# A recurrent scan feeding two layers of experts: units one iteration earlier, their lists counted at step 1 and made in fewer steps

## The chip, the cores and the metric

One core of one Trainium2 chip runs the whole program. The metric is the device time of one execution in microseconds (us): the median of several executions. The core's engines are TensorE (PE in the rows; PEld is its weight loading), VectorE (DVE), ScalarE (ACT), GpSimd (POOL) and SyncE (SP, which here issues DMA transfers). Each works through its own queue in order and waits on the others by semaphores.

## What is computed

A gated recurrence over four sequences of 5056 tokens with 256 channels, then two layers of experts. In the first layer only tokens with a positive score are sent to an expert, in the second all are.

```python
# scan
f = lower_bound + (1 - lower_bound) * sigmoid(f_logit)
for t in range(S):                       # S = 5056, B = 4, D = 256
    h = f[:, t] * h + (1 - f[:, t]) * x[:, t];  y[:, t] = h
# layer 1, N = B*S = 20224 tokens, 8 experts, F = 1024
go = x @ w_skip > 0
e  = argmax(x[go] @ w_gate);  g = softmax(x[go] @ w_gate)[e]
out[go] = x[go] + g * (relu(x[go] @ w1[e]) @ w2[e]);  out[~go] = x[~go]
# layer 2, all tokens
e  = argmax(x @ w_gate2);  g = softmax(x @ w_gate2)[e]
out = g * (relu(x @ w1b[e]) @ w2b[e])
```

## The kernel before

**Chunks and iterations.** The scan runs over 40 chunks of 512 tokens, in a software pipeline of iterations `i` of four steps `s` = 0 to 3 (`side` and `work`). In an iteration VectorE scans a chunk (`scan2`, line 856), TensorE turns one to token rows (`turn`, line 880) and multiplies one by the gates' weights (`logits`, line 908; 923 and 926 from chunk 20 on), and every second iteration a group of eight tiles of 128 tokens is routed (`route`, odd iterations) and placed (`place`, even iterations): TensorE ranks the group's tokens within their experts (`ps_rank`), VectorE adds the group to the running count of tokens per expert (line 985), and GpSimd scatters the rows to a region per expert in memory (line 274), two tiles a step.

**Units.** A unit is 256 tokens of one expert (128 for the last, small ones). `Moe.step(k)` is a quarter of a unit: four steps make one, `k = 4u + f`. In step f TensorE does 12 products of the first matrix (`mm1`, line 609: hidden block f, in three half-precision parts) and, for the hidden block of two steps before, 12 of the second (`mm2`, lines 637 to 639). ScalarE and VectorE split each hidden block in two halves (`hh` line 620, `hl` line 621). At f = 2 the next unit's rows are transposed (`xpose`: `ps_x` line 596, then `xh` line 597 on ScalarE and `xl` line 598 on VectorE); at f = 3 the rows of the unit after that are loaded by SyncE (`load`, line 564). A unit's last `mm2` is done at f = 1 of the next, and VectorE then adds it to the rows (`finish1`, line 645). The step ends with `side(k)`, a quarter of an iteration of the scan, at s = f. Before unit 0 the scan runs alone for `I0` iterations; after the scan the units run alone. There are 126 units in all.

**Lists.** Which rows a unit takes is computed on the chip. At iteration 12, 16, 20, ... 40 `lists_of_scan(e)` starts list e with four units each. `count` multiplies the running count by ones (line 326, `ps_c`), so that every partition has the sum, and VectorE takes it over (line 329). Lists 0 and 1 then need two instructions (lines 535, 536); lists 2 to 7 some 20 small ones on tiles of 8 numbers (lines 407 to 493), a product with ones (`ps_b`, line 499) and two copies (501, 507). These steps are slipped in between the scan's instructions: `tick` after a step of a generator of `work`, the rest at a step's end by `listing`, up to `LS[s]` of them in step s; products only in steps named in `PS`. `state.cnt` in `count` is whatever count line 985 made last.

**Queues and buffers.** All orders are the order in which the program is written. `ps_x`, `ps_t`, `ps_l`, `ps_c` and `ps_b` share one pool of two PSUM buffers (`pt`), and `ps_o` of `mm2` a pool of three. Experts' weights are loaded and split meanwhile by `weights`, on the two schedules `WI`/`WS` before unit 0 and two a iteration after; the last eight quarters (from number 24 on) go over GpSimd (line 191).

**After the scan** (iteration 42, step 3) the small lists of layer 1 are made, rows of finished units are sorted into the regions of layer 2 and scattered by GpSimd (`sort_some`), and units run on.

Of the kernel before, what the change touches and what calls it, by code (L numbers as in the profile page):

```python
# [31 lines left out]
NU = (NT + E * (UT - 1)) // UT  # L32


I0, LN, NEARLY, K1A, K1B = 16, 4, 8, 6, 4
K2E, K2A, K2B = 8, 70, 6
NFIX = E // LN
NSCAN = LN * NEARLY * UJ
# [5 lines left out]
DL, DB, UF, KL = 2, 3, 5, 11  # L44

WQ = [(e, k) for e in range(E) for k in (2, 3)] + [(e, k) for e in range(E) for k in (0, 1)]
WI, WS, WD = [1, 2, 1] * 5 + [1], [1, 3], 0
WL = 17
WT = 24
LG, LB, LA1 = 4, 3, 1  # L50
CK, CS = 4, 3
KS, KX = 7, 3
CF = 20
LA, LF = 2, 3
LS = (8, 8, 10, 10)
PS = (3, 0, 1)

WB, LT, LT2, UW = 2, 6, 5, 4
# [36 lines left out]
def moe_chain(ctx: ExitStack, tc: tile.TileContext, xT, fT, lb, wg, w1a, w2a, w1b, w2b, out):  # L95
# [646 lines left out]
    with ExitStack() as ph:  # L742
# [677 lines left out]
        def side(k):  # L1420

            i, s = divmod(k + 4 * I0, 4)
            if k == -KS:
                moe.begin(units, n)
                moe.start()
            GL.n = LS[s]
            if i < nchunk + 3:
# [93 lines left out]
```

## Time and profile before

| | us |
|---|---|
| median of three executions (1580.51 to 1587.67) | 1583.88 |
| the profiled execution, its own time | 1587.33 |
| its span, first to last instruction | 1585.6 |
| TensorE busy in the span | 1498.6 |
| VectorE busy | 925.5 |
| ScalarE busy | 725.0 |
| GpSimd busy | 507.9 |

The span falls into three parts. Up to 140 us the scan runs alone, 140 to about 510 us scan and units run together, and from there on only units and sorting. TensorE is the engine with the most work. A gap in its row is time lost only where no other part of the program makes up for it, so its gaps are looked up one by one with what ended them. A row of the timeline gives the start in us from the span's begin, the duration, the engine, the line and the operation, and in brackets how long the engine stood idle before and what released it; rows of equal instructions that follow each other are merged (x2).

### The profile page before, as it was taken

The numbers are of one execution on the slowest core, as the hardware profiler recorded it, in microseconds if no ns is written. First come the engines' busy times: TensorE is split into PE (matmuls) and PEld (weight loads), VectorE is DVE, ScalarE is ACT, GpSimd is POOL, SyncE is SP. The second block draws the span as 40 slices with busy tenths as digits, with TensorE's granted clock in tenths as the row PEclk, the third lists the DMA queues.
The fourth block names the chain that finished last, engine by engine and source line by source line (L and its number), as shares of the span: only waits on it lengthen the run. The fifth ranks groups of instructions, "written<-read, shape, count | busy, mean of one in ns | idle before, by whom it ended". The sixth has DMA issues, their size and how long they took to land. (4 is left out here: it accounts for less than half of the span.)

```text
span 1585.6 us, 41240 instructions
## 1 busy us (share of the span) xinstructions
PE 1498.6 (95%) x13900; PEld 1346.4 (85%) x13901; DVE 925.5 (58%) x1947; ACT 725.0 (46%) x1419; POOL 507.9 (32%) x511
## 2 busy tenths in 40 slices
PE   5878989999999998999999999999999999999996
PEld 5877868888988887887888998998989989989985
DVE  5877677888885865546755555544444444444442
ACT  6777567776763232333344443433333333333332
POOL 1663455646453177016111111111111111111121
PEclk9988989999999999999999999999999999999998
DMA  8876655777774377327333323111111111111110
GB/s 289 274 266 212 212 178 201 260 243 252 242 253 153 103 232 244 121 71 243 110 100 103 97 98 106 50 49 56 49 50 57 47 51 50 49 54 49 49 48 22
DMA packets 127221, 213.73 MB, mean 135 GB/s; under 512 B 14459, under 2 KB 87807, under 8 KB 124464
## 3 DMA queue, kind: packets, MB, share of 16 engines
q1 hardware_dynamic: 107824, 157.51, 31.5%
q0 software_dynamic: 19200, 53.53, 9.2%
q8 instruction: 132, 2.16, 0.6%
q14 instruction: 65, 0.53, 0.1%
HBM read 120.10 MB, written 70.80 MB: 120 GB/s over the span
## 5 line engine op out<-in xcount | busy, mean ns | idle before, releaser
L621 DVE SCALAR_TENSOR_TENSOR hl<-ps_m,hh 128x512 f16<-128x512 f32 (+1 forms) x504 | 336.9, 668 | 554.6 <-ACT hh L620 553.1
L620 ACT ACTIVATE hh<-ps_m 128x512 f16<-128x512 f32 (+1 forms) x504 | 292.2, 580 | 634.8 <-PE ps_m L609 527.3
L637 PE MATMUL ps_o<-wt,hh 128*128 (+2 forms) x1936 | 531.7, 275 | 8.4 <-DVE rows L645 8.4
L638 PE MATMUL ps_o<-wt,hh 128*128 (+2 forms) x1936 | 531.8, 275 | 0.0
L639 PE MATMUL ps_o<-wt,hl 128*128 (+2 forms) x1936 | 531.7, 275 | 0.0
L609 PE MATMUL ps_m<-xh,w1s 128*128 128x256 f16 (+1 forms) x2880 | 505.9, 267 | 0.0
L609 PEld LDWEIGHTS <-w1s 128*128 128x128 f16 x4320 | 406.7, 98 | 45.5 <-issue 0.4
L274 POOL DMA_INDIRECT out_dram<-rows,dest x162 | 157.6, 973 | 750.1 <-ACT rows L681 636.8
L609 PE MATMUL ps_m<-xl,w1s 128*128 128x256 f16 (+1 forms) x1440 | 378.6, 267 | 0.0
L638 PEld LDWEIGHTS <-hh 128*128 128x128 f16 x1936 | 190.0, 98 | 33.5 <-issue 9.3
L609 PE MATMUL ps_m<-xh,wt 128*128 128x256 f16 x1152 | 215.9, 276 | 2.4 <-DVE hl L621 2.4
L639 PEld LDWEIGHTS <-hl 128*128 128x128 f16 x1936 | 190.1, 98 | 25.0
L637 PEld LDWEIGHTS <-hh 128*128 128x128 f16 x1936 | 190.0, 98 | 22.6
L274 POOL DMA_INDIRECT regions<-rw,dest x158 | 175.9, 1113 | 91.9 <-issue 42.5
L609 PEld LDWEIGHTS <-wt 128*128 128x128 f16 x1728 | 168.8, 99 | 23.8 <-issue 3.1
L609 PE MATMUL ps_m<-xl,wt 128*128 128x256 f16 x576 | 158.7, 276 | 0.0
L583 DVE COPY w1s<-wt 128x4096 f16 x90 | 110.8, 1231 | 11.6 <-issue 4.8
L274 POOL DMA_INDIRECT regions<-wt,b_dest x80 | 84.7, 1059 | 42.2 <-issue 17.9
L856 DVE TENSOR_TENSOR_SCAN xt<-ft,end,xt 128x512 f32<-128x512 f32 (+4 forms) x78 | 94.9, 1246 | 0.4
L598 DVE SCALAR_TENSOR_TENSOR xl<-ps_x,xh 128x512 f16<-128x512 f32 (+1 forms) x126 | 83.1, 660 | 16.7 <-ACT xh L597 16.6
L596 PE MATMUL ps_x<-ident,rows 128*128 128x128 f32 x484 | 75.0, 276 | 18.2 <-DMA rows<-regions 18.2
L681 ACT ACTIVATE rows<-ps_o,rows 128x256 f32<-128x256 f32 x162 | 68.3, 471 | 33.2 <-PE ps_o L639 33.2
(241 smaller groups left out, 1317.1 us busy)
## 6 DMA issues: line engine op xcount, KB each, us to landing
rows<-regions SPq DMA_DIRECT2D x116, 272.0 KB, 2.8
wt<-wt SPq DMA_DIRECT2D x20, 1024.0 KB, 6.0
ft<-in_fT_dram SPq DMA_DIRECT2D x39, 512.0 KB, 4.0
xt<-in_xT_dram SPq DMA_DIRECT2D x39, 512.0 KB, 4.9
wt<-mid SPq DMA_DIRECT2D x40, 272.0 KB, 4.5
mid<-rows SPq DMA_DIRECT2D x38, 272.0 KB, 3.6
wt<-in_w2a_dram SPq DMA_DIRECT2D x16, 512.0 KB, 4.7
wt<-in_w1a_dram SPq DMA_DIRECT2D x16, 512.0 KB, 3.9
```

Of the source, the lines that this page charges most:

```text
L274: r = nc.gpsimd.indirect_dma_start(out=dst, out_offset=bass.IndirectOffsetOnAxis(ap=idx_ap, axis=0), in_=rows_ap, in_offset=None, bounds_c ...
L583: nc.vector.tensor_copy(t.w1, wt[:, bass.ds(o, W2O)])
L596: nc.tensor.transpose(ps[:, d, j * P : (j + 1) * P], t.rows[:, j, d * P : (d + 1) * P], ident)
L598: nc.vector.scalar_tensor_tensor(out=t.xl, in0=ps, scalar=SX, in1=t.xh, op0=ALU.mult, op1=ALU.subtract)
L609: nc.tensor.matmul(ps[:, f, :], lhsT=t.w1[:, wo : wo + P], rhs=x[:, d, :], start=f == 0 and k == 0, stop=f == 1 and k == 5, skip_group_che ...
L620: nc.scalar.activation(hh, ps, AF.Relu)
L621: nc.vector.scalar_tensor_tensor(out=hl, in0=ps, scalar=0.0, in1=hh, op0=ALU.max, op1=ALU.subtract)
L637: nc.tensor.matmul(ps, lhsT=hh[:, f, js], rhs=hi, start=first, stop=False)
L638: nc.tensor.matmul(ps, lhsT=hh[:, f, js], rhs=lo, start=False, stop=False)
L639: nc.tensor.matmul(ps, lhsT=hl[:, f, js], rhs=hi, start=False, stop=last)
L681: nc.scalar.activation(y, t.ps[j][:, :D], AF.Copy, scale=t.rows[:, j, CGATE : CGATE + 1])
L856: nc.vector.tensor_tensor_scan(x[:, d, s0:s1], f[:, d, s0:s1], x[:, d, s0:s1], init, ALU.mult, ALU.subtract)
```

## The change

Four constants are changed, and the shape of one.

```diff
-I0, LN, NEARLY, K1A, K1B = 16, 4, 8, 6, 4
+I0, LN, NEARLY, K1A, K1B = 15, 4, 8, 6, 4
...
-WI, WS, WD = [1, 2, 1] * 5 + [1], [1, 3], 0
+WI, WS, WD = [1, 2, 1] * 5, [1, 3], 0
...
-CK, CS = 4, 3
+CK, CS = 3, 1
...
-LS = (8, 8, 10, 10)
+LS = (12, 12, 12, 12)
```

`I0`: unit u runs in iteration 15 + u instead of 16 + u; all that hangs on a unit (its load, its transposition, the lists after the scan, the sorting) keeps its place relative to the unit or to the iteration as the code has it. `WI` loses the entry of iteration 15, which now follows the schedule of iterations with units: two quarters of weights are handled in it instead of one, and all later ones one call earlier. `CK`, `CS`: list e is begun in the same iteration, 12 + 4e, but at step 1 instead of step 3; its first unit is in iteration 15 + 4e instead of 16 + 4e. At step 1 of these iterations line 985 has just been issued, so the same groups are counted as before. `LS`: up to 12 instead of 8 or 10 list steps in a step.

The first units on TensorE. Before, the count's transposed unit rows (`ps_x`) and the first `mm1` of unit 0 (`ps_m`) stand behind the gates' product `ps_l` of chunk 13:

```order
L233 MATMUL ps_rank<-oh,ones 128x128
L1037 MATMUL ps_v<-wgt,wt 128x48 x8
L880 MATMUL ps_t<-ident,xt 128x128 x8
L908 MATMUL ps_l<-wgt,xt 128x102 x8
L596 MATMUL ps_x<-ident,rows 128x128 x4
L880 MATMUL ps_t<-ident,xt 128x128 x8
L609 LDWEIGHTS wt
L609 MATMUL ps_m<-xh,wt 128x256
```

with the change:

```order
L233 MATMUL ps_rank<-oh,ones 128x128
L1037 MATMUL ps_v<-wgt,wt 128x48 x8
L596 MATMUL ps_x<-ident,rows 128x128 x4
L880 MATMUL ps_t<-ident,xt 128x128 x8
L609 LDWEIGHTS wt
L609 MATMUL ps_m<-xh,wt 128x256
```

The product `ps_l` of that chunk now stands behind the first step of unit 0, and one iteration of the scan that had no unit beside it has one.

The count on TensorE in iteration 24, the fourth of eight (`ps_c` is the count, the rows with `waits` name the semaphore that is waited for). Before, it stands at the end of step 3, behind the gates' product:

```order
L926 MATMUL ps_l<-wg_114,ft 128x17
L326 LDWEIGHTS ones
L326 MATMUL ps_c<-oh,ones 128x8 [waits DVE_49]
L609 LDWEIGHTS wt [waits DMAHW1_49]
L609 MATMUL ps_m<-xh,wt 128x256
```

With the change it stands at the end of step 1, straight behind the last product of `mm2`, and its weight load waits for VectorE:

```order
L639 LDWEIGHTS hl
L639 ISA
L639 MATMUL ps_o<-wt,hl 128x264
L326 LDWEIGHTS ones [waits DVE_49]
L326 MATMUL ps_c<-oh,ones 128x8 [waits Activation_49]
L609 LDWEIGHTS wt
L609 MATMUL ps_m<-xh,wt 128x256 [waits PE_49]
```

Twelve products, the four transpositions `ps_x` and twelve products later, the transposition of the scan waits for VectorE too:

```order
L639 LDWEIGHTS hl
L639 ISA
L639 MATMUL ps_o<-wt,hl 128x264
L880 MATMUL ps_t<-ident,xt 128x128 [waits DVE_49]
L880 MATMUL ps_t<-ident,xt 128x128 x3
L609 LDWEIGHTS wt
L609 MATMUL ps_m<-xh,wt 128x256
```

What moved is the count alone; before, `ps_t` of that step waits for none of VectorE's instructions of the list.

The list on VectorE in the same iteration. Before, line 329 and the list's steps stand behind and between the scans of iteration 25, ahead of `hl` and of `rows` (line 645, the next row):

```order
L329 TENSOR_TENSOR V_125<-ps_c,start_104 128x8
L856 SCALAR_TENSOR_TENSOR xt<-ft,end,xt 128x512
L407 TENSOR_TENSOR ni<-V_125,base_128 128x8
L413 TENSOR_SCALAR ni<-ni 128x8
L418 CAST nu<-ni 128x8
L422 SCALAR_TENSOR_TENSOR ue<-ones_94,nu 128x8
L426 TENSOR_TENSOR us<-ue,nu 128x8
L428 TENSOR_SCALAR t<-ue,tokid 128x8
L431 SCALAR_TENSOR_TENSOR t<-us,tokid,t 128x8
L432 SCALAR_TENSOR_TENSOR V_125<-us,base_128 128x8
L435 TENSOR_SCALAR us<-us 128x8
L621 SCALAR_TENSOR_TENSOR hl<-ps_m,hh 128x512
```

With the change they stand in step 2 of iteration 24, behind the placing of the group, `hl` and `xl`:

```order
L985 TENSOR_REDUCE oh<-oh 128x16
L240 TENSOR_TENSOR d<-ps_rank,oh 128x128
L243 TENSOR_REDUCE df_3664<-d 128x8
L246 SCALAR_TENSOR_TENSOR dest<-df_3664 128x8
L621 SCALAR_TENSOR_TENSOR hl<-ps_m,hh 128x512
L598 SCALAR_TENSOR_TENSOR xl<-ps_x,xh 128x512
L329 TENSOR_TENSOR V_125<-ps_c,start_104 128x8
L407 TENSOR_TENSOR ni<-V_125,base_128 128x8
L413 TENSOR_SCALAR ni<-ni 128x8
L418 CAST nu<-ni 128x8
L422 SCALAR_TENSOR_TENSOR ue<-ones_94,nu 128x8
L426 TENSOR_TENSOR us<-ue,nu 128x8
```

All but the last three instructions of the list (470, 480, 493) now follow in one run before the next `hl`; the product `ps_b` comes at step 0 instead of step 3 of iteration 25.

## Rows read from the trace of the kernel before

**Rows 1.** the page, part 1: engine, busy us, share of the span, instructions

```profile
PE 1498.6 (95%) x13900; PEld 1346.4 (85%) x13901; DVE 925.5 (58%) x1947; ACT 725.0 (46%) x1419; POOL 507.9 (32%) x511
```

**Rows 2.** window: start:end, length, busy us (PE, PEld, DVE, ACT, POOL), clock, DMA

```profile
250.00:510.00 260.00, 256.15 (x2594) 228.72 (x2593) 204.42 (x517) 173.97 (x338) 141.63 (x122) 1.00 0.69 237
```

**Rows 3.** TensorE's waits, 140 to 510 us: waiter, releaser: us in total, times, longest

```profile
PE ps_o L637 <- DVE rows L645: 7.0, 4, 4.4
...
PE ps_l L923 <- ACT rw L883: 5.3, 6, 1.6
```

**Rows 4.** timeline of TensorE, iterations 14 to 16: start, us, instruction, [idle before <-releaser]

```profile
132.02 3.74 PE L908 MATMUL ps_l<-wgt,xt 128*128 128x102 f32 x16 [2.42 <-ACT rw L883]
...
140.43 0.36 PE L609 MATMUL ps_m<-xh,wt 128*128 128x256 f16 x1
...
146.80 0.38 PE L609 MATMUL ps_m<-xh,wt 128*128 128x256 f16 x2
...
160.64 0.27 PE L609 MATMUL ps_m<-xh,wt 128*128 128x256 f16 x1
```

**Rows 5.** timeline of VectorE, iterations 14 and 15, then the window from there

```profile
130.57 2.41 DVE L185 SCALAR_TENSOR_TENSOR wt<-wt 128x1024 f16<-128x1024 f32 x2 [0.75 <-ACT wt L184]
132.90 1.21 DVE L844 SCALAR_TENSOR_TENSOR xt<-ft,xt 128x1024 f32<-128x1024 f32 x1
...
144.59 2.45 DVE L856 TENSOR_TENSOR_SCAN xt<-ft,end,xt 128x512 f32<-128x512 f32 x2
...
133.00:160.60 27.60, 25.02 (x199) 22.26 (x199) 21.87 (x38) 17.72 (x36) 11.81 (x11) 0.86 0.63 211
```

**Rows 6.** instructions of line 596 on TensorE, 1000 to 1400 us: four a unit

```profile
L596 PE MATMUL ps_x<-ident,rows x148: 272/273/273, 1003.8 to 1397.1; 128*128 128x128 f32 x148
```

**Rows 7.** timelines of iteration 28: TensorE, then VectorE, then TensorE and GpSimd

```profile
324.46 0.27 PE L609 MATMUL ps_m<-xh,wt 128*128 128x256 f16 x1
...
325.40 0.41 DVE L985 TENSOR_REDUCE oh<-oh 128x16 f16<-128x144 f16 x1
...
326.36 2.14 DVE L246 SCALAR_TENSOR_TENSOR dest<-df 128x8 uint32<-128x8 f32 x1
...
329.25 0.68 DVE L598 SCALAR_TENSOR_TENSOR xl<-ps_x,xh 128x512 f16<-128x512 f32 x1
...
327.55 0.60 PE L880 MATMUL ps_t<-ident,xt 128*128 128x128 f32 x4
...
326.35 2.13 POOL L893 TENSOR_TENSOR ft<-xt,ft 128x1024 f16<-128x1024 f32 x1 [5.84 <-DVE df L243]
```

**Rows 8.** timelines of iteration 21 (VectorE, GpSimd, TensorE), then the window round it

```profile
227.28 2.85 DVE L435 TENSOR_SCALAR us<-us 128x8 f32<-128x8 f32 x1
...
227.96 2.14 POOL L191 TENSOR_TENSOR wt<-wt 128x1024 f16<-128x1024 f32 x1
...
231.18 0.38 PE L637 MATMUL ps_o<-wt,hh 128*128 128x264 f16 x1 [4.42 <-DVE rows L645]
...
226.00:238.00 12.00, 7.39 (x44) 5.51 (x43) 10.00 (x30) 5.58 (x9) 10.46 (x10) 0.72 0.43 152
```

**Rows 9.** timelines of iteration 20 (TensorE, GpSimd): first product, end of a weight split

```profile
201.67 0.27 PE L609 MATMUL ps_m<-xh,wt 128*128 128x256 f16 x1
...
201.84 2.14 POOL L191 TENSOR_TENSOR wt<-wt 128x1024 f16<-128x1024 f32 x1
```

**Rows 10.** waits of SyncE's queue, 560 to 645 us

```profile
SPq L564 <- DMA regions<-wt,b_dest: 41.0, 7, 7.6
```

**Rows 11.** timeline of TensorE at two gaps, then windows that hold them

```profile
596.30 0.44 PE L596 MATMUL ps_x<-ident,rows 128*128 128x128 f32 x2 [2.73 <-DMA rows<-regions]
...
608.44 0.47 PE L596 MATMUL ps_x<-ident,rows 128*128 128x128 f32 x1 [2.61 <-DMA rows<-regions]
...
593.00:600.00 7.00, 4.27 (x39) 3.44 (x37) 2.85 (x8) 1.40 (x5) 5.23 (x6) 1.00 0.75 230
605.00:615.00 10.00, 7.39 (x66) 6.34 (x64) 3.50 (x11) 2.51 (x8) 7.45 (x8) 0.83 0.88 273
```

## The prediction

> **What bounds the kernel now.** I read the page first: TensorE is busy 1498.6 us of the 1585.6 us span [rows 1]. Then the windows, since that share is a mean over stages: from 250 to 510 us, with scan and units side by side, TensorE is busy 256.15 of 260 us at a granted clock of 1.00 [rows 2]. There, any wait that TensorE gets is paid in full, and any that it loses is won. Third, its waits between 140 and 510 us [rows 3]: four times for `rows` (line 645, 7.0 us in all, one of them 4.4) and six times for the copies of `ps_t` (line 883, 5.3 us). Fourth, what stands ahead of these waits in the timelines. The 4.42 us are in iteration 21 [rows 8]: VectorE there has the list's steps ahead of `rows`, one of which (435) took 2.85 us. Of the 5.3 us about 4.8 lie in the four iterations that make a list, where the scan's instructions come late by the list's steps among them; I leave 0.5. Before 140 us the order on VectorE and ScalarE sets the pace: the gates' product of chunk 13 begins at 132.02 after 2.42 us of idle time, and unit 0's first product only at 140.43 [rows 4].
>
> **The earlier start.** Iteration 15 now has unit 0 beside it, and one iteration that ran alone is gone. Take as mark the second unit's products of step 2: 160.64 us before [rows 4]. With the change VectorE decides when they come, as TensorE has less to do. In the order of the changed kernel VectorE has, from 133.0 us (the end of the pair of weight splits that begins at 130.57) to the count of iteration 16, what it had between 133.0 and 160.6, 21.87 us [rows 5], without the last two scans (2.45), one weight split (2.41 / 2 = 1.2), one product of line 844 (1.21) and the placing (some 0.8), but with two more `hl` and one `rows` (together about 2.3, each `hl` taken like the 0.68 of line 598 [rows 7]). That is 21.9 - 5.7 + 2.3 = 18.5, so 151.5; for TensorE to answer, and for the wait for the count in that very iteration, I add 0.9: 152.4, or 8.2 us sooner than before. One scan iteration's work is still to be done beside a later unit. Unit 0 and unit 1 lay 160.64 - 146.9 = 13.7 us apart [rows 4]; a unit alone takes (1397.1 - 1003.8) / 36 = 10.9 us [rows 6], since 148 instructions, four a unit, lie 36 periods apart. So 2.8 us come back: **-5.4 us**. Bounds: -8 if the rest finds gaps, -2.5 if the granted clock is low there longer than before (0.86 in that window [rows 5]) or ScalarE, with 17.72 us of work in it, holds the chain. I take a value near the first, as VectorE has the larger sum.
>
> **The count's wait.** `ps_c` now stands directly behind the 12 products of `mm2` of step 1, and its weight load waits for line 985 of the same step. Behind it in TensorE's queue are the 12 `mm1` and four `ps_x` of step 2, hence `hh`, `hl` and `xl`, and all that follows. The trace of before has no such wait; I bound it by iteration 28 [rows 7]. Line 985 ends there at 325.40 + 0.41 = 325.81, while the first `mm1` of step 2 began at 324.46: with `ps_c` (0.1) in between TensorE stands 1.45 us. Then `mm1` 1.31, `ps_x` 0.43 and `mm2` 1.34 follow (their spacing before), up to about 329.0, and the transposition `ps_t` follows, which has no PSUM buffer of its own any more: `ps_c` holds one until VectorE reads it (line 329, behind `xl`), so it waits for `xl` to give back the other. `xl` ended at 329.25 + 0.68 = 329.93 in a VectorE queue that was already held up by line 246 (2.14 us). So `ps_t` begins near 330.05 and not at 327.55: 2.5 us. Read in the same way, iterations 20 and 24 give 2.6 each, 32 and 36 2.5 each, and 40, without a transposition in step 2, 1.45. Together 2.6 + 2.6 + 2.5 + 2.5 + 2.5 + 1.45 = **+14.1 us** (iteration 16 is in the term above). Bounds: 6 x 1.45 = 8.7 where `xl` is never late, 17 where the later `mm1` pushes `xl` by another 0.5 each time.
>
> **The list's new place.** Line 329 and some 18 list steps leave the odd iterations and stand in step 2 of the even ones, behind `hl` and `xl`. What they cost there on VectorE is about 3 us, ahead of `hl` of step 3; in iteration 28 they would end near 332.8 (`xl` ends at 329.93 [rows 7]). The reader of that `hl` is line 639 two steps on, which stood at 335.71 in the same timeline and comes 1.45 us or more later now, so not ahead of 337: less the 0.7 of `hl` itself, 3.4 us are to spare. So the list costs nothing there, and would cost up to 3 us a time if this cover were gone. What they release: the 4.8 us of line 923's waits, 4.42 - 0.5 = 3.9 us of iteration 21, and the fall of the clock behind it. The window of 226 to 238 us has a granted clock of 0.72 [rows 8], that is 0.28 x 12 / 0.5 = 6.7 us at the lower level (1.2 GHz); the work done in them would take half as long at 2.4, so between nothing and 3.35 us, of which I take two thirds, 2.3, as the engine was not busy throughout. Sum **-11.0 us**, bounds -6 (nothing of the clock, a new wait half as long in place of the old) and -12.
>
> **Weights, rows and sorting.** The splits of experts' weights keep their iterations while units move one ahead. In iteration 20 a split on GpSimd ends at 201.84 + 2.14 = 203.98, and the unit that will then need it, now a whole unit earlier, has its first product where another had it at 201.67 [rows 9]. Its products of this part come about 1.1 us into its step: **+1.2 us** (0 to 2.3). On SyncE the loads of rows of units 0 and 1 now pass `f` and `x` of chunk 14; each is one transfer of rows that nobody reads before the next iteration: nothing. After the scan the loads that wait for the scatter, 41.0 us in seven times on SyncE's queue [rows 10], start relative to another unit; that may go either way by what one gap of TensorE there shows, 2.73 us at 596.30 [rows 11], and I take 0 (-2 to +2).
>
> **Sum:** -5.4 + 14.1 - 11.0 + 1.2 = -1.1 us, against the profiled execution's 1587.33. That execution is 3.45 above the median of 1583.88, and the difference carries over: 1582.8, and as the unmeasured parts of the list's new place lean upwards (its bounds are +5 and -1 round the value) I say **1584 us: no change**. Half a per cent, 7.9 us, is about what a measurement of this kernel can tell from no change.
>
> **Rivals.** *The counts are hidden after all* (faster). In iterations 16 to 22 VectorE and ScalarE are the slower engines, as 21.87 us in 27.6 [rows 5] and the waits in [rows 3] show; a wait of TensorE there only moves its idle time, and the products behind catch up. Then of the counts only those of 28 to 40 cost something, and at their lower bound: 4 x 1.45 = 5.8 rather than 14.1, and the start brings 8 rather than 5.4. Against it speaks that from 250 us on nothing is left to catch up in. Sum -5.4 - 2.6 + 5.8 - 11.0 + 1.2 = -12.0: **1572 us**.
>
> *The clock falls behind each new wait* (slower). After the gap of 2.61 us at 608.44 the granted clock in the window of 605 to 615 is 0.83, so 0.17 x 10 / 0.5 = 3.4 us at the lower level and some 1.7 us lost; after a gap of 2.73 us at 596.30 the window of 593 to 600 has 1.00 [rows 11]. A count now makes two gaps a few us apart, 1.45 and 1.0, with a run of products between them. If the clock falls after each of the seven, 7 x 1.7 = 11.9 us come on top of 1584: **1596 us**. It decides from five of the seven on. For it speaks iteration 21's fall, against it that each gap alone is shorter than either of these two, and that one of the two left the clock at its upper level.
>
> *The start brings nothing:* iteration 15 with a unit lasts as long as 15 and 16 did together, since `hl`, `xl` and the scan's instructions must take turns on VectorE. The sum is then +4.3 instead of -1.1, so 1584 + 5.4: **1589 us**, still no change.
>
> *VectorE and GpSimd get in each other's way in the new place.* Line 435 took 2.85 us while GpSimd's split of 2.14 us ran [rows 8], and line 246, 2.14 us with the halves of line 893, 2.13 us, begun 0.01 us before [rows 7]: small instructions lasted as long as GpSimd's large one. In the list's new place line 893 has ended at 328.48, and the list begins near 329.9. A hit would cost VectorE 2.1 us of the 3.4 to spare, so it shows only where something else is late as well; with that in half of six iterations, 3 x 2.1 = 6 us, **1590 us**. The Trainium skill ("SBUF — State Buffer", "Who interferes with whom") has this as a rule: VectorE and GpSimd share one pair of ports under an exclusive lock, whoever issues first has it for the whole instruction, and the other is fully blocked. By that rule every hit would last as long as GpSimd's instruction, and the sum would be this rival's; the trace's two rows agree with it.
>
> **How the numbers follow.** Forecast 0.47 (no change); counts hidden 0.23 (faster); clock 0.20 (slower); start brings nothing 0.06 and ports 0.04 (no change, though 0.03 of these two lies beyond the bound together with a second mishap, slower). Faster 0.23, same 0.54, slower 0.23. The forecast's own bounds add up to about 1575 and 1594 where two terms go one way; the range takes in both large rivals with it, 1570 to 1597.
>
> **What would show it.** In the profile after: unit 0's first product near 132, not 140; line 326 on TensorE with about 1.4 us idle before it, released by VectorE, in seven iterations, and `ps_t` behind it with about 1 us; no gap of 4.4 us at the second list and no waits of line 923 near lists; a clock of 1.00 round iteration 21; TensorE's busy time unchanged. The forecast is wrong if the counts' waits are short because line 985 comes early (its place on VectorE behind `rows`), or if they pull the clock down; a start that is not 5 us earlier at the second unit's step 2 breaks the first term.

## The result: slower by one per cent, where no change was forecast

The changed kernel takes 1605.26 us (median of 6, 1598.07 to 1609.20) where the kernel before takes 1584.85 (1579.92 to 1587.67): a ratio of 1.0126, 95% interval 1.0098 to 1.0154. A second measurement (e10, below) gave 1.0102 (1.0050 to 1.0153). The forecast was 1584 with a range of 1570 to 1597: the result lies 8 us above the range.

The page of the changed kernel, its first part (engine, busy us, share of the span, instructions), answers to [rows 1]:

```profile
PE 1506.9 (94%) x13900; PEld 1351.6 (84%) x13901; DVE 937.7 (59%) x1946; ACT 726.7 (45%) x1419; POOL 507.4 (32%) x511
```

TensorE has as many instructions as before, 13900, and is busy 8.3 us longer in a span that is 16.3 us longer: half of the loss looks like work. It isn't: in a second pair of traces (e9 and e10, below) it is busy 14.0 us shorter in the changed kernel (1494.6 for 1508.6). The busy time follows the mean granted clock of the execution, whichever the kernel: 1494.6 us at 0.980, 1498.6 at 0.979, 1506.9 and 1508.6 at 0.973. So a reading by stages is needed, and it has to tell the clock from waits. TensorE's waits between 140 and 512 us (waiter, releaser: us in total, times, longest), the answer to [rows 3]:

```profile
PE ps_c L326 <- DVE oh L985: 8.6, 7, 1.2
...
PE ps_m L609 <- POOL wt L191: 4.4, 2, 3.3
PE ps_t L880 <- DVE xl L598: 3.8, 7, 0.8
```

None of the three was there before; the two that were, for `rows` and for the copies of `ps_t` ahead of line 923, are gone (e10 has one of 0.7 us ahead of line 923). Iteration 28 of the changed kernel, TensorE, VectorE and GpSimd, answers to [rows 7]:

```profile
344.87 0.18 PE L326 MATMUL ps_c<-oh,ones 128*128 128x8 f16 x1 [1.25 <-DVE oh L985]
348.98 0.66 PE L880 MATMUL ps_t<-ident,xt 128*128 128x128 f32 x4 [0.82 <-DVE xl L598]
...
344.41 0.40 DVE L985 TENSOR_REDUCE oh<-oh 128x16 f16<-128x144 f16 x1
...
345.37 2.14 DVE L246 SCALAR_TENSOR_TENSOR dest<-df 128x8 uint32<-128x8 f32 x1
...
348.25 0.68 DVE L598 SCALAR_TENSOR_TENSOR xl<-ps_x,xh 128x512 f16<-128x512 f32 x1
348.84 0.16 DVE L329 TENSOR_TENSOR V<-ps_c,start 128x8 f32<-128x8 f32 x1
...
345.35 2.13 POOL L893 TENSOR_TENSOR ft<-xt,ft 128x1024 f16<-128x1024 f32 x1 [5.89 <-DVE df L243]
```

This is the predicted chain: the count waits for line 985, and `ps_t`, four microseconds on, for `xl`, with line 329 (which gives the count's buffer back) right behind `xl`. Ahead of `xl` stands line 246, which takes 2.14 us here and 0.17 where GpSimd's line 893 isn't begun at the same moment. Between 140 and 520 us it is held in this way eight times in either trace of the changed kernel and three times in either trace of the kernel before.

The time by stages, worked out from the timelines. "Chunk 10" is the row of line 864 on ScalarE that ends the scan of chunk 10; "unit j" is the first row of line 596 that transposes unit j's rows, in step 2 of the unit before. Two traces of either kernel (e9 is the kernel before, e10 the changed one, each taken again, both on one chip), us:

| stretch | before | e9 | after | e10 | mean change |
|---|---|---|---|---|---|
| start to chunk 10 (the same program) | 97.2 | 107.1 | 103.5 | 96.7 | (chance) |
| chunk 10 to unit 2 | 64.8 | 65.0 | 67.2 | 67.7 | +2.5 |
| unit 2 to unit 8 | 99.7 | 89.9 | 96.3 | 96.2 | +1.5 |
| unit 8 to unit 28 | 254.7 | 254.9 | 261.4 | 262.0 | +6.9 |
| unit 28 to the end | 1069.1 | 1069.0 | 1073.6 | 1075.2 | +5.4 |

The first line needs a word. Up to there the two programs are equal, and yet four traces lie 10 us apart. The windows of its first 97 us, the kernel before in e9 and the changed one in e10 (start:end, length, busy us of PE, PEld, DVE, ACT and POOL, granted clock, DMA share, GB/s):

```profile
0.00:97.00 97.00, 74.41 (x504) 71.86 (x506) 65.23 (x135) 66.57 (x135) 37.15 (x61) 0.82 0.80 263
```

```profile
0.00:97.00 97.00, 70.05 (x571) 67.65 (x573) 70.16 (x142) 71.30 (x148) 43.44 (x65) 0.95 0.84 277
```

A granted clock of 0.82 in one execution and 0.95 in the other: how long the lower level (1.2 GHz) lasts in the first 100 us differs from execution to execution. The 6.3 us that the first pair of traces shows there say nothing about the change, and single traces of this kernel can't be compared by their spans. The four lines under it can, and they add up to +16.3 us; the medians of the two pairs lie 20.4 and 14.7 us apart.

### The profile page after: what moved, and what is told of

It reads as the page before. It is cut to its first block, busy times and chain, and to the rows that moved or that the text cites. A ratio compares the mean times of both kernels' runs of the same rounds, so it can differ in the third digit from the quotient of the medians.

```text
span 1601.9 us, 41235 instructions
## 1 busy us (share of the span) xinstructions
PE 1506.9 (94%) x13900; PEld 1351.6 (84%) x13901; DVE 937.7 (59%) x1946; ACT 726.7 (45%) x1419; POOL 507.4 (32%) x511
## 3 DMA queue, kind: packets, MB, share of 16 engines
q8 instruction: 132, 2.16, 0.6%
## 5 line engine op out<-in xcount | busy, mean ns | idle before, releaser
L609 PEld LDWEIGHTS <-w1s 128*128 128x128 f16 x4272 | 402.5, 98 | 45.6 <-issue 0.4
L609 PE MATMUL ps_m<-xl,w1s 128*128 128x256 f16 (+1 forms) x1424 | 374.7, 267 | 0.0
L609 PE MATMUL ps_m<-xh,wt 128*128 128x256 f16 x1184 | 220.8, 275 | 7.2 <-POOL wt L191 4.4
L274 POOL DMA_INDIRECT regions<-rw,dest x158 | 171.8, 1087 | 96.1 <-issue 42.7
L609 PE MATMUL ps_m<-xl,wt 128*128 128x256 f16 x592 | 162.4, 274 | 0.0
L596 PE MATMUL ps_x<-ident,rows 128*128 128x128 f32 x484 | 74.9, 276 | 18.4 <-DMA rows<-regions 18.3
```

What stands on the lines that cost most here:

```text
L274: r = nc.gpsimd.indirect_dma_start(out=dst, out_offset=bass.IndirectOffsetOnAxis(ap=idx_ap, axis=0), in_=rows_ap, in_offset=None, bounds_c ...
L596: nc.tensor.transpose(ps[:, d, j * P : (j + 1) * P], t.rows[:, j, d * P : (d + 1) * P], ident)
L609: nc.tensor.matmul(ps[:, f, :], lhsT=t.w1[:, wo : wo + P], rhs=x[:, d, :], start=f == 0 and k == 0, stop=f == 1 and k == 5, skip_group_che ...
```

## The experiments

All ratios are to runs of the kernel before on the same chip. e1 to e18 used four chips: on two of them the kernel before takes 1585 us (e1 to e4; e9 to e12), on the others 1611 to 1613 (e5 to e8, e17 and e18; e13 to e16). What differs there is told at the end; stretches are compared on chips of one kind.

**Which part loses? e1 to e4.**

e1 moves the loads of the rows of units 0 and 1 two steps on:

```diff
-KS, KX = 7, 3
+KS, KX = 5, 3
```

> The changed kernel with one constant altered: units 0 and 1 load their rows two steps later (KS 5 instead of 7: step 3 of iteration 13 instead of step 1), behind f and x of chunk 14 and the weights of step 1 in SyncE's queue. Theory A (that load waits 9.2 us for the scatter of the group that was placed one iteration before, and f, x and an expert's weights wait behind it): the 6.15 us that ScalarE waits for weights in iteration 13 go, and 1605 falls by 5 to 9 us, to 1596 to 1600. Rival B (the loss is made by the counts that TensorE waits for): no change, 1605. Rival C (the first 100 us ran at a lower clock by chance, 6 us): 1605 as well, and the time from the start to chunk 10's scan differs from run to run while the program is the same there.

Measured: 1597.88 us, ratio 1.0075 (1.0045 to 1.0104). What the loads did in the changed kernel, SyncE's waits from 110 to 160 us, its rows there, and ScalarE's first wait for weights:

```profile
SPq L564 <- DMA regions<-rw,dest: 9.2, 1, 9.2
```

```profile
127.43 0.88 SPq L564 DMA_DIRECT2D rows<-regions  x2
128.42 0.40 SPq L829 DMA_DIRECT2D ft<-in_fT_dram  x1
128.92 0.41 SPq L824 DMA_DIRECT2D xt<-in_xT_dram  x1
129.44 2.05 SPq L1012 DMA_DIRECT2D wt<-in_w1a_dram  x2
...
136.92 1.06 ACT L184 ACTIVATE wt<-wt 128x1024 f16<-128x1024 f32 x1 [6.15 <-DMA wt<-in_w1a_dram]
```

The load waits 9.2 us for the scatter of the rows of the group that was placed just before, and holds `f`, `x` and an expert's weights behind it; ScalarE then stands 6.15 us for these weights. In the kernel before the same load follows the weights ahead of it without a wait, at

```profile
124.76 0.94 SPq L564 DMA_DIRECT2D rows<-regions  x2
```

In e1 it still waits 5.4 us, but behind the `f`, the `x` and the weights that it held up. ScalarE's waits for such weights in e1 are, from 110 to 150 us:

```profile
ACT wt L184 <- DMA wt<-in_w1a_dram: 2.2, 2, 1.9
```

and the stretch from chunk 10 to unit 2 is 63.7 us instead of 67.2 and 67.7. That is 3.7 us for theory A, less than the 5 to 9 that it expected; the ratio fell by 0.003 to 0.005 (4 to 8 us), and the greater part of the loss stayed.

e2 and e3 keep the earlier start, but count later (e2; e3 has CS 2 and LA 2):

```diff
-CK, CS = 3, 1
+CK, CS = 3, 3
-LA, LF = 2, 3
+LA, LF = 1, 3
-PS = (3, 0, 1)
+PS = (0, 1, 2, 3)
```

> The earlier start with the lists counted at step 3 as before (CS 3; so that they are ready in time, products are allowed in every step, PS 0 to 3, and wait one call, LA 1). Theory B: the seven waits of TensorE for line 985 (8.6 us in all) and the seven for xl (3.8 us) go, the list's steps come back to the odd iterations and cost 4 to 6 there: 1605 falls by 5 to 8, to 1597 to 1600. Theory A alone: the loads' place is untouched, so the 9.2 us wait on SyncE's queue stays and the time is within 3 us of 1605.

> The earlier start with the count one step later (CS 2, PS 0 to 3): the product stands behind TensorE's work of step 2, when line 985 is long done, and ps_t of step 2 stands ahead of it and has its own buffer. Theory B: the waits for line 985 and xl vanish (12.4 us together in the trace of the changed kernel), of which 8 to 12 come back, 1593 to 1597, if the list's steps in step 3 and step 0 delay nothing; 1600 if they delay the scan as they did before. Theory A alone: within 3 us of 1605.

Measured: 1.0232 (1.0175 to 1.0289) and 1.0200 (1.0141 to 1.0258), 14 to 18 us slower than the changed kernel, where both were to be faster. Neither isolates the count: to have the list ready in time its product had to be allowed everywhere, and TensorE now waits for the list itself, in e2

```profile
PE ps_b L499 <- DVE vbe L493: 27.7, 5, 7.9
```

In e3 that wait is 8.2 us, and `ps_t` waits for `xl` all the same, 15.3 us in five waits. What follows is only that the earlier start needs the earlier count; units that start an iteration sooner, with lists counted at step 3 or 2, lose 34 to 38 us to the kernel before.

e4 is the other half of the change alone, the lists without the earlier start:

```diff
-CK, CS = 4, 3
+CK, CS = 4, 1
-LS = (8, 8, 10, 10)
+LS = (12, 12, 12, 12)
```

> The kernel before with the list part of the change alone (count at step 1, up to 12 list steps a step), units still from iteration 16. Theory B: per four iterations 1.1 us more, as between units 8 and 24 of the changed kernel (52.8 for 51.7 us), and 2 to 3 us at iteration 12, so 1585 + 8 to 10: 1593 to 1595. Theory A: the loss belongs to the earlier start, so 1585 within 4 us.

Measured: 1596.89 us, 1.0075 (1.0043 to 1.0107), 12 us and a little over what theory B said. From unit 8 to unit 28 it takes 261.9 us, as the changed kernel does: the steady loss is the lists' alone. From unit 28 to the end it takes 1069.6, as the kernel before: that loss is the start's alone. And from chunk 10 to unit 2 it takes 68.6 for 64.9: the lists of iterations 12 and 16 have their price too.

**What in the count? e5 to e8, e11, e12.** e5 is e4 with line 985 issued one step sooner (in `work`, s = 0), so that the count finds it done:

```diff
-                    take(G[2], 1)
+                    take(G[2], 2)
```

> The kernel before with the list part of the change (count at step 1, up to 12 list steps) as in e4, and line 985 issued one step sooner (step 0 instead of step 1 of the same iteration; the same groups are counted, TensorE's order is the same). Theory B1 (of the 12 us that e4 lost, the price is TensorE's wait for line 985): its 11.6 us in seven waits go to nearly 0, the waits for xl (3.7 us) may stay, and 1597 falls by 8 to 12 to 1585 to 1589. Rival B2 (the loss is the list's steps in their new place on VectorE): 1597 within 3.

Measured: 1.0074 (1.0047 to 1.0101), no better. The waits of e4 and, behind them, of e5:

```profile
PE ps_c L326 <- DVE oh L985: 11.6, 7, 3.7
...
PE ps_t L880 <- DVE xl L598: 3.7, 6, 0.8
```

```profile
PE ps_t L880 <- DVE xl L598: 12.0, 7, 2.5
...
PE ps_c L326 <- DVE oh L985: 1.7, 1, 1.7
```

The wait for line 985 went and came back as a wait for `xl`: 15.3 us together in e4, 13.7 in e5. So B1 falls as it was put. The first wait only stood ahead of the second. Nor is it line 246, which is held eight times in e4 and never in e5.

e6 is the changed kernel with the same line moved, e7 that with KS 5, e8 that with UF 4 (the first lists of layer 2 one unit later).

> The changed kernel with line 985 issued one step sooner, all else unchanged. Theory B1: 8.6 us of waits in seven go, so 1605 falls to 1595 to 1598; the load of units 0 and 1 still blocks SyncE's queue and ScalarE still waits some 6 us for weights in iteration 13. Rival B2: 1605 within 3.

> The changed kernel with both: line 985 a step sooner, and the rows of units 0 and 1 loaded at step 3 (KS 5). If the two causes add up (7 us by e1, 8 to 10 by e6): 1605 - 16 = 1589, within 3 of e5, which has the same list but starts an iteration later: the start then is worth nothing. If the start brings the 5 us that were predicted once it is free of the load's wait: 5 us under e5.

> The kernel of e7 with the first lists of layer 2 begun one unit later (UF 4 instead of 5), so that they stand to the end of the scan as they did before the change. Theory D (in all kernels that start from iteration 15 the stretch from unit 28 to the end took 4 to 6 us longer in the profile, at units 39 to 41, since the sorting begins a unit later and the loads wait for its scatter): 2 to 5 us under e7. Rival (that stretch varies by chance, or is bound by the sort itself): within 2 of e7.

Measured: 1.0085 (1.0062 to 1.0108), 1.0068 (1.0044 to 1.0092) and 1.0106 (1.0072 to 1.0141). e6, from which B1 took 7 to 10 us, lies 3 to 7 under the changed kernel by the ratios. e7 was to be at 1589 us if the two causes added up; it is where e5 is (1.0068 and 1.0074), so with the count's buffer unmended the earlier start is worth nothing. e6 and e7, which differ in the load of units 0 and 1 alone, differ by 0.0017, less than their intervals, and by 2.6 us from chunk 10 to unit 2 (64.4 and 61.8): theory A once more. e8 was to be faster than e7 and is 0.0038 slower.

e11 is e5 with the count's product in the pool of `ps_o` (in `count` and `lists_of_scan`):

```diff
-        ps = ps_pool.tile([P, E], F32, tag="px", name="ps_c")
+        ps = ps_pool.tile([P, E], F32, tag=tag, name="ps_c")
...
-            GL.todo += [count(ul, pt, S1), g]
+            GL.todo += [count(ul, po, S1, tag="po"), g]
```

> The kernel of e5 (units from iteration 16, lists begun at step 1, line 985 a step sooner), with the count's product in a PSUM buffer of the pool of ps_o (three buffers) instead of the pool that it shares with ps_x and ps_t (two). Theory E (e5 traded 8.6 us of waits for line 985 for 8 us more of waits for xl, since the count holds one of two buffers until VectorE reads it behind xl): the waits of ps_t for xl, 12.0 us in e5, fall under 2, nothing takes their place, and the ratio falls from 1.0074 to 0.997 to 1.000. Rival F (VectorE is late in these steps whatever TensorE waits for; hl or rows takes the place of xl): 1.005 to 1.008.

Measured: 1582.76 us, 0.9976 (0.9949 to 1.0004). Its waits, TensorE, 140 to 512 us:

```profile
PE ps_t L880 <- ACT rw L883: 5.0, 2, 4.1
PE ps_c L326 <- DVE oh L985: 2.8, 2, 2.3
```

No wait for `xl` is left, nothing of size took its place, and from unit 8 to unit 28 it takes 253.1 us: 8.8 less than e4 and 1.7 less than the kernel before. Theory E holds. With line 985 early the price of the count is the buffer: `ps_c` holds one of two that the transpositions need, until VectorE reads it behind `xl`. On the chip of e5, e17 (the same kernel as e11) gave 0.9977 (0.9958 to 0.9995): 0.0097 under e5, 15 us for one buffer, and line 246 is held in neither of the two. The buffer alone, with line 985 in its old place, was not run, so how the changed kernel's own loss divides between the wait for line 985, the holds of line 246 and the buffer isn't shown.

> The kernel of e11 once more (units from iteration 16, count early and in its own buffer), since e11 and e13 ran on chips on which the kernel before takes 1585 and 1611 us. All theories of the count: 0.9976 again, 0.995 to 1.000.

So e11 is ahead of the changed kernel by more than one per cent, and of the kernel before by a quarter of one, just clear of noise in e17 and not in e11.

e9 and e10 are the kernels before and after once more; e12 is e7 with the count in the pool of `ps_o`, all three on the chip of e11.

> The kernel before once more, for its trace on the same chip as the next three (e5 to e8 ran on a chip on which it took 1611 us). Every theory: ratio 1.000; the time from the start to the scan of chunk 10, where all kernels are the same program, is a matter of the execution and lies anywhere between 97 and 106 us, as in the traces so far.

> The changed kernel once more, on the same chip as e9. Every theory: ratio 1.010 to 1.015; its waits again 8 to 9 us for line 985, 4 for xl and 9 on SyncE's queue in iteration 13.

> The kernel of e7 (earlier start with the rows of units 0 and 1 loaded at step 3, line 985 a step sooner) with the count's product in the pool of ps_o. Theory E: from 1.0068 to 0.998 to 1.001. If the earlier start, free of its two new waits, brings the 5 us that were predicted: 0.003 under e11. Rival: equal to e11, as what is gained at the start is given back behind the scan. Rival F: 1.005 to 1.007.

Measured: 1.0008 (0.9979 to 1.0036), 1.0102 (1.0050 to 1.0153) and 1.0013 (0.9987 to 1.0038). The buffer helps the earlier start as well, by 0.0055 against e7 on another chip, but e12 is not better than e11: by the ratios it is 6 us behind it, by the medians 3.

**Where does the start's gain go? e13 to e16, e18.** By stretches, e11, e12, and two kernels of the next group that ran on a chip of the other kind, on which only the first stretches may be compared:

| stretch | e11 | e12 | e14 | e15 |
|---|---|---|---|---|
| chunk 10 to unit 2 | 67.0 | 60.7 | 62.6 | 64.8 |
| unit 2 to unit 8 | 89.9 | 97.3 | 90.9 | 96.9 |
| unit 8 to unit 28 | 253.1 | 254.0 | | |
| unit 28 to the end | 1068.6 | 1076.8 | | |

The start does bring 6.3 us by unit 2 (e12 against e11), and more than that is lost behind it: 7.4 us to unit 8 and 8.2 behind unit 28. (The traced execution is the slowest of e12's eleven, 1595.22 us, so its stretches may be longer than usual.) e15 is e12 with KS 7 again; e14 is e12 with a quarter of weights more ahead of unit 0:

```diff
-WI, WS, WD = [1, 2, 1] * 5, [1, 3], 0
+WI, WS, WD = [1, 2, 1] * 4 + [1, 2, 2], [1, 3], 0
```

> The kernel of e12 with the rows of units 0 and 1 loaded at step 1 of iteration 13 as the change has it (KS 7). Theory A: the wait on SyncE's queue is back, the time from the scan of chunk 10 to the load of unit 2's rows grows by 4 to 7 us, and the ratio from 1.0013 to 1.004 to 1.006. Rival: within 0.001 of e12.

> The kernel of e12 (units from iteration 15, both new waits mended) with one more quarter of weights handled before unit 0: the last entry of WI is 2 instead of 1, so every later quarter comes one call, half an iteration, sooner. Theory G (with the earlier start the first products of units 5 and 7 wait for GpSimd's split of weights, 4.4 us in two waits in e12, and the clock falls behind them, 13 us at the lower level): the waits for POOL wt go, the stretch from unit 3 to unit 8 falls from 83.6 us to 76 to 78, and the ratio from 1.0013 to 0.997, if iteration 14, which gets the work, doesn't lose it again. Rival: TensorE stands there for the list or the clock anyway: within 0.001 of e12.

Measured: e15 1.0034 (1.0009 to 1.0059), a little under the 1.004 to 1.006 that theory A expected, and 64.8 us to unit 2 against 60.7 in e12: theory A again, 4.1 us across two chips. SyncE's row of e15 from 100 to 170 us:

```profile
SPq L564 <- DMA regions<-rw,dest: 17.0, 2, 8.9
```

e14: 0.9998 (0.9972 to 1.0023). Its waits have no line for GpSimd's split any more, which in e12 (and with 4.4 and 4.7 us in the two traces of the changed kernel) is

```profile
PE ps_m L609 <- POOL wt L191: 4.4, 2, 3.5
```

and unit 2 to unit 8 falls from 97.3 and 96.9 us to 90.9. Theory G holds for the stretch, 6.2 us, and misses the ratio of 0.997 that it expected. By ratio, e14 is 0.0036 under e15, from which it differs by both edits (2.2 us in the first stretch, since the quarter of weights takes some 2 us back in iteration 14, and 6.0 in the second); 5.8 of these 8.2 us show in the ratio. e14 is the changed kernel with the load, the count and the weights mended, and it is back at the time of the kernel before.

e13 is e11 with the sorting begun a unit later (`sort_some` from iteration 44 on), e18 the same on the chip of e17; e16 is e14 with the turn to sorting two steps sooner.

> The kernel of e11 (units from iteration 16) in which the sorting behind the scan begins one unit (four steps) later; the lists behind the scan stay where they are. In the six traces that start from iteration 15 on these chips the stretch from unit 28 to the end takes 1073.6 to 1076.8 us, in the four that start from iteration 16 it takes 1068.6 to 1069.6. Theory D (that is since the sorting begins a unit later relative to the units, and the loads of units 33 to 41 wait for its scatter): this stretch grows to 1073 to 1077 with the start untouched, and the ratio from 0.9976 to 1.001. Rival (it is another thing of the earlier start): the stretch stays within 1068 to 1070, ratio 0.9976.

> The kernel of e14 in which the turn from scan to sorting (the lists behind the scan, and the sorting with them) comes two steps sooner, at step 1 of iteration 42, with what is left of the scan's scatters issued there at once. Theory D: two steps of the four come back, so the stretch from unit 28 to the end is 2 to 4 us shorter than in e14, and the ratio 0.001 to 0.002 under e14's, 0.995. Rival: no shorter, or longer, since the scatters queue up in one step.

> The kernel of e13 (the sorting begun one unit later) on the same chip as e17. Theory D: 4 to 7 us over e17 (a ratio higher by 0.0025 to 0.0045), and all of it in the stretch from unit 28 to the end. Rival: within 2 us of e17, and the 5 us that this stretch is longer in every kernel with the earlier start have another cause.

Measured: e13 0.9999 (0.9979 to 1.0019) on another chip than e11, hence e18: 0.9974 (0.9952 to 0.9997) against 0.9977 for e17 beside it. e16: 1.0015 (0.9992 to 1.0038), not faster than e14. By the medians theory D falls: e18 is no slower than e17, where 4 to 7 us were expected, and a turn two steps sooner brings nothing. The traces say otherwise. From unit 28 to the end e17 takes 1079.1 us and e18 1084.9, the 5.8 us of theory D. But e5 and e17, which both start at iteration 16 with the sorting in its old place, differ by 6.7 us there as well, and the test was not made on a chip of the kind on which the loss was seen. The two answers don't agree, and the matter stays open.

Every kernel with the earlier start takes 4 to 8 us longer behind unit 28 (1073.6 to 1076.8 us in six traces, against 1068.6 to 1069.6 in four that start at iteration 16; all on chips of one kind). The traces show where. Units 28 to 31 take 48.9 us instead of 47.8, since they have the times that units 27 to 30 had: 12.65, 12.87, 12.03 and 11.32 us for 12.64, 12.87, 12.03 and 11.30. What stood beside a unit now stands beside the next. And units 39 and 40, which wait for sorted rows, take together 19.9 to 23.9 us in those six traces and 16.9 to 18.5 in those four. With the sorting begun late and the start untouched they take 23.5 us (e13) and 21.1 (e18), on the same kind of chip 16.8 without (e5, e17); e15, with the earlier start, has 18.3 there. So this part goes with the sorting's place in most traces; why the median of e18 doesn't show it stays open.

## Why the prediction was wrong, step by step

**The earlier start, -5.4.** This step failed most. By its own mark the gain was to be 8.2 us, with unit 0's first product near 132 us instead of 140.43. The changed kernel has it at

```profile
146.46 0.42 PE L609 MATMUL ps_m<-xh,wt 128*128 128x256 f16 x1
```

which is 43.0 us behind chunk 10 (42.7 in e10), where both traces of the kernel before have 43.3; and by unit 2 there is a loss of 2.5 us. The order on VectorE, from which the 8.2 was worked out, holds in part: freed of the rest, the start brings 6.3 us (e12 against e11, which has the same lists), or 4.2 against the kernel before. What failed is the sentence on SyncE, "each is one transfer of rows that nobody reads before the next iteration: nothing". It asked who reads these loads and not what they wait for, and who is queued behind them: 2.6 to 4.1 us (e1, e6 against e7, e15). The second hole is the list of iteration 12, which the sum left out, as no unit runs beside it. `ps_c` waits for line 985 there too,

```profile
112.43 0.19 PE L326 MATMUL ps_c<-oh,ones 128*128 128x8 f16 x1 [2.50 <-DVE oh L985]
```

with the gates' and the weights' products behind it. e4 loses 3.7 us by unit 2, of which the count of iteration 16 with a wait of 1.74 us has a part; in e11, where that wait is 0.55 and this one still 2.50, 2.1 us are lost. The rest of the way from -8.2 to +2.5 stays open.

**The count, +14.1, and the list's new place, -11.0.** For iterations 24 to 40 this was 1.3 us too high. The counts' terms there are 2.6 + 3 x 2.5 + 1.45 = 11.55. Of the 4.8 us that were to go with line 923, which the prediction put into four iterations, 1.42 lie in iteration 21, ahead of unit 8,

```profile
239.23 0.18 PE L923 MATMUL ps_l<-wg,ft 128*128 128x34 f16 x1 [1.42 <-ACT rw L883]
```

and 3.3 in the four behind it. So +8.2 was booked, and unit 8 to unit 28 measures +6.9, all of it by the lists (e4). The waits themselves are smaller than forecast: 6.2 us for line 985 and 3.3 for `xl` in these five iterations. The mechanism, a count that holds a buffer until VectorE reads it behind `xl`, was named in the prediction and is shown by e5, e11 and e17 for the kernels with line 985 early. For iteration 21 the term was wrong: the 4.42 us of idle time and the fall of the clock behind it [rows 8] aren't there in every execution. In the second trace of the kernel before, the wait for `rows` in that iteration is

```profile
231.11 0.27 PE L637 MATMUL ps_o<-wt,hh 128*128 128x264 f16 x1 [0.22 <-DVE rows L645]
```

line 435 takes 0.26 us where [rows 8] have 2.85, and the stretch takes 89.9 us instead of 99.7. Of the 6.2 us that were booked as gained there, that execution had next to nothing to give.

**The split of weights, +1.2.** Mis-sized: 4.4 us in two waits, the second of 3.29 us at 258.42 that the prediction didn't look for, and the clock beside them. The windows 216 to 228 and 256 to 268 of the changed kernel:

```profile
216.00:228.00 12.00, 8.41 (x51) 6.37 (x49) 9.21 (x16) 9.09 (x14) 8.45 (x6) 0.72 0.52 187
256.00:268.00 12.00, 9.58 (x78) 8.00 (x79) 9.25 (x13) 4.93 (x9) 3.94 (x4) 0.86 0.62 221
```

with a granted clock of 0.72 and 0.86. e14 takes them away and gets 6.2 us back. Unit 2 to unit 8 is so +1.5 in the mean, where the sum had -2.4, or -3.8 with line 923's 1.4.

**Behind the scan, 0.** +5.4 measured, outside the -2 to +2. The prediction had an iteration's work of 2.8 us come back "beside a later unit"; 1.1 of the 5.4 lie in units 28 to 31, whose times have moved by one unit, and most of the rest in units 39 and 40. Whether the sorting's place is its cause stays open.

**The rivals.** That the counts would be hidden fell where it weighs most: from unit 8 on they are paid. For iteration 20 it may hold. The changed kernel has a wait of 1.2 us for line 985 there, e12 and e15 have none, and unit 2 to unit 8 takes 96.3 and 96.2 us in its two traces and 97.3 and 96.9 in theirs. That the clock would fall behind the counts fell too. The window of the changed kernel from 250 to 510 us, an answer to [rows 2],

```profile
250.00:510.00 260.00, 247.09 (x2497) 218.62 (x2496) 218.62 (x499) 176.58 (x339) 140.91 (x118) 0.99 0.68 232
```

has a granted clock of 0.99, and 1.00 from 270 us on; the fall in it is where GpSimd's split is waited for. VectorE and GpSimd didn't collide in the list's new place: iteration 28's list runs from 348.84 to 351.6 with each instruction at 0.14 to 0.23 us. They did ahead of it, at line 246, five times more than before. (Of the two rows that the prediction took as agreeing with the rule on ports, line 435's begins 0.68 us ahead of GpSimd's split, 227.28 and 227.96, and ends with it; it doesn't show who was first.) The third rival, a start that brings nothing, is near what the stretch to unit 2 shows, but not for its reason: e1, with the same order on VectorE, has unit 0's first product 38.6 us behind chunk 10 instead of 43.0. The count was the forecast's own mechanism. The load and the split were missed because a step that moved was followed on TensorE and VectorE and not in the queues of SyncE and GpSimd.

## What to carry to other kernels

When work starts an iteration sooner, list for every load and every scatter of it what it waits for at the new place, and what stands behind it in the same queue; a load that nobody is in a hurry to read can still block one that somebody is. When a wait is to be taken away, look for the next one behind it, and for the buffer that links them: e5 removed 10 us of waits and won nothing, e11 moved 8 numbers to another PSUM pool and won 15. And price a stall from more than one trace where the program has stretches whose clock is a matter of the execution.

## What the runs showed of the hardware

Line 246 on VectorE (128x8) takes 0.17 us when it begins 0.1 to 0.35 us ahead of GpSimd's line 893 (128x1024). In every one of the 55 times in all traces in which it began 0.01 to 0.07 us behind, it took 2.08 to 2.16, as long as line 893. It was so held in every kernel with line 985 in its old place, and in none with line 985 a step sooner.

The same program runs at different clocks in its first 100 us: from the start to chunk 10's scan 96.7 to 107.1 us over all traces here. The window of 0.95 above is 0.05 x 97 / 0.5 = 10 us at the lower level, that of 0.82 is 35 us.

The chips differ. On two of them the kernel before takes 1585 us, on the other two 1611 to 1613, and the program of e11 takes 1583 and 1609. Of the 23.9 us between the traces of e11 and e17, the same program, 22.4 lie between unit 8 and unit 49 (unit 28 to 49: 237.0 and 247.8), while the stretch behind it, where units run alone, is equal (831.7 and 831.2). The two longest of TensorE's waits from 520 to 700 us in e17, and then the longest of the kernel before on the other kind of chip:

```profile
PE ps_m L609 <- issue: 8.2, 10, 3.5
PE ps_m L609 <- DVE hl L621: 6.7, 5, 3.9
```

```profile
PE ps_x L596 <- DMA rows<-regions: 11.3, 7, 2.7
```

Time in which TensorE waited for nothing that the profile shows takes the place of the waits for rows. What it is stays open; against the 1.6 to 1.8 per cent between the chips, the 0.2 to 1.3 per cent of this case are only seen in ratios on one chip.
